# Fourier mixing and a gated feed-forward: the 481-column chunk goes first, and its half row tiles are joined over two batches

## The chip, the core and the metric

One core of a Trainium2 chip runs the kernel. The metric is the device time of one execution in microseconds (us). Engines are named as in the profile: PE is TensorE (matmuls; PEld its weight loads), DVE is VectorE, ACT is ScalarE, POOL is GpSimd, SP is SyncE, whose queue issues nearly all DMAs. SBUF is the on-chip memory, PSUM the small memory that matmuls write. POOL's work here lies in SBUF alone.

## The reference

The input `x` is 8 batches of 3008 tokens with 256 values. The reference mixes by a Fourier transform and sends every token through a gated feed-forward block:

```python
X = np.fft.fft(x, axis=1)
X = np.fft.fft(X, axis=2)
x = X.real.reshape(24064, 256)
g = x @ w_gate                              # 256 x 1536
gelu = 0.5 * g * (1.0 + erf(g / sqrt(2)))
out = (gelu * (x @ w_val)) @ w_out          # 1536 x 256
```

## The kernel before

**Half the tokens, twice used.** The transform is built so that token t and its mirror 3008 - t come from one column: an even part and an odd part, added for t (called plus) and subtracted for the mirror (minus). Instead of 3008 tokens the first layer therefore works on NCOL = 1505 columns of a tile Y with two planes. The channel transform is folded into the weights WE (even), WOP (odd) and WOM (odd, negated). Column 1504 is a token that is its own mirror: it has a plus and no minus.

**Chunks and units.** A batch's 1505 columns are cut into three chunks (line 73) of 512, 512 and 481 columns, in this order. The hidden dimension of 1536 is cut into 12 blocks. A unit is one chunk and one block, so a batch has 36 units and the run 288; units are counted from 0 within a batch below. In a unit PE runs five first-layer matmuls (six in the first chunk of batch 0): WE into the value bank ps_v, WOM of the unit before into its gate bank ps_g, WOP of the unit before into its value bank, and WE and WOP into this unit's gate bank. ACT takes the gelu twice, glp for plus and glm for minus.

**Who writes h.** The hidden values of a chunk go into a tile h of 12 blocks with 1024 columns each. h has two buffers, so a chunk's tile takes over that of the chunk before last. Units go in pairs, and a pair is finished in the unit behind it: `val_odd` (line 628) has DVE multiply glp with the value bank into the plus columns of h (two blocks, 128x1024), then DVE computes dv, the minus value, and `minus` (line 647) has POOL multiply glm with dv into the minus columns, mirrored. Ahead of these DVE has one `ev` per unit, which reads ps_v between its two matmuls. In the first chunk of batch 0 DVE writes the minus columns too. Plus columns start at 0 in a block and minus columns at 512, for all three chunks.

**The second layer.** `l2_steps` (line 659) makes the list of matmuls of a finished chunk: four windows of plus columns and then four of minus columns, each of up to 128 tokens and each with 12 matmuls (one per block) of 256 output columns. The 481 chunk's last plus window has 97 tokens and its last minus window 96. Two windows share a PSUM tile ps_o of 512 columns, which has one buffer; after a pair's 24th matmul `finish` (line 701) has ACT copy it to SBUF (osb, two buffers) and SP store it by runs of 32 rows. In the last chunk of the run the pairs go to ps_o, ps_d, ps_g and ps_g.

**The order.** Each engine runs its instructions in the order in which the program issues them, by the loop at line 817. A unit's body issues the first layer, then steps of the next batch's transform (`a_step`, `b_steps`, which ACT evacuates), and last `second(8)` (line 916): eight second-layer matmuls from the list. The list of chunk c is added in the unit behind its last one, after that unit's `minus`, and 96 matmuls last 12 units. So in units 12 to 23 of a batch the second layer of its first chunk runs under the first layer of its second chunk; in units 24 to 35 that of the second chunk; and in units 0 to 11 that of the last batch's third chunk. POOL's queue also holds the folding of later batches' input (`fold_x`), in some of the odd units.

The output columns of the transform reach Y in two evacuations per step, `evac_top` (line 533, columns 0 to 767) and `evac_rest` (line 541, columns from 768 on).

Of the kernel before, what the change touches and what calls it, by code (L numbers as in the profile page):

```python
# [10 lines left out]
BF16 = mybir.dt.bfloat16  # L11
AF = mybir.ActivationFunctionType
# [25 lines left out]
def kernel(  # L38
# [20 lines left out]
    nc = tc.nc  # L59
# [10 lines left out]
    NFC = F // 128  # L70
    NCOL = T // 2 + 1
    YW = NCOL + 1
    CH = [(0, 512), (512, 512), (1024, NCOL - 1024)]
    MID = 24

    const_pool = ctx.enter_context(tc.tile_pool(name="const", bufs=1))
# [18 lines left out]
    WNb = const_pool.tile([128, NFC], BF16)  # L95
    WN = const_pool.tile([128, NFC], FP32)
    NQs = [const_pool.tile([128, YW], BF16, name=f"nq{i}") for i in range(2)]
    xf_bufs = [const_pool.tile([128, HJ, 2, 128], BF16, name=f"xf{i}") for i in range(2)]

    Ap = const_pool.tile([128, NG, C], BF16)  # L100
# [88 lines left out]
    def ps_d():  # L189
        return psum.tile([128, 512], FP32, tag="d", bufs=1, name="ps_d")  # L190
# [307 lines left out]
    def b_steps(b, eo, q):  # L498
# [40 lines left out]
                _sub(ps, [[1, MID], [N2, 8]], 0))  # L539

        def evac_rest():
            ps, Y, g0 = box["ps"], Ys[b], 8 * q
            n2 = N2 - MID
            f = 1 if q == 0 else 0
            copy(
                _sub(Y, [[32, n2], [1, 8 - f]], eo * YW + 32 * MID + g0 + f - 1),
                _sub(ps, [[1, n2], [N2, 8 - f]], MID + f * N2))
            if q == 0:
                copy(
                    _sub(Y, [[32, n2]], eo * YW + 32 * MID + 31), ps[:, MID:N2])  # L550
                copy(
                    _sub(Y, [[1, 1]], eo * YW + NCOL - 1), ps[:, 8 * N2 : 8 * N2 + 1])

        steps = [mm(gi, False) for gi in range(8)]
        if eo == 1 and b == 0:
            steps += [mm(gi, True) for gi in range(8)]
        def evac():
            evac_top()
            evac_rest()

        return steps, evac, evac_top, evac_rest

# [12 lines left out]
    def open_unit(u):  # L575
        b, ci, fc = units[u]
        if fc == 0:
            hs[(b, ci)] = h_tile()
        c0, n = CH[ci]
        if u % 2 == 0:  # L580
            duos[u // 2] = dict(pv=ps_v(), glp=glp_tile(), glm=glm_tile(), log=[])
            if kind(u):
                duos[u // 2]["ev"] = ev_tile()
        banks[u] = dict(
            d=duos[u // 2], k=u % 2, pv=duos[u // 2]["pv"][:, u % 2, :],
            glp=duos[u // 2]["glp"][:, u % 2, :], glm=duos[u // 2]["glm"][:, u % 2, :],
            b=b, fc=fc, c0=c0, n=n, nm=n - n % 32, kd=kind(u), fs=slice(fc * 128, (fc + 1) * 128),
            h=hs[(b, ci)], Y=Ys[b], nq=NQs[b % 2])

    def layer1(r, ps, W, i, eo, n, start):  # L590
        m = pe.matmul(
# [31 lines left out]
    def plus(r):  # L623
        n = r["n"]
        apart(r["d"]["log"], r["k"], vec.tensor_tensor(
            r["h"][:, r["fc"], :n], r["glp"][:, :n], r["pv"][:, :n], op=ALU.mult))

    def val_odd(u):
        r = banks[u]
        n, nm, d = r["n"], r["nm"], r["d"]  # L630
        if r["kd"] == 0:
            layer1(r, r["pv"], WOM, 1, 1, nm, False)
            hm = _sub(r["h"], [[-1, nm]], r["fc"] * 1024 + 512 + nm - 1)
            apart(d["log"], r["k"], vec.tensor_tensor(
                hm, r["glm"][:, :nm], r["pv"][:, :nm], op=ALU.mult))
            return
        layer1(r, r["pv"], WOP, 1, 1, n, False)
        if r["k"]:
            f = r["fc"] - 1
            apart(d["log"], None, vec.tensor_tensor(  # L640
                r["h"][:, f : f + 2, :n], d["glp"][:, :, :n], d["pv"][:, :, :n], op=ALU.mult))
            d["dv"] = dv_tile()
            apart(d["log"], None, vec.scalar_tensor_tensor(
                d["dv"][:, :, :nm], d["ev"][:, :, :nm], 2.0, d["pv"][:, :, :nm],
                op0=ALU.mult, op1=ALU.subtract))

    def minus(u):
        r = banks.pop(u)
        if r["kd"] and r["k"]:
            nm, d = r["nm"], r["d"]  # L650
            hm = _sub(r["h"], [[1024, 2], [-1, nm]], (r["fc"] - 1) * 1024 + 512 + nm - 1)
            pool.tensor_tensor(hm, d["glm"][:, :, :nm], d["dv"][:, :, :nm], op=ALU.mult)

    def store(b, dst_row, t, p0, s0, ns, rows, step):
        dst = ap_replace(
            out, ap=[[C, rows], [step * C, ns], [1, C]], offset=out.offset + (b * T + dst_row) * C)
        nc.sync.dma_start(out=dst, in_=_sub(t, [[C, ns], [1, C]], s0 * C, p0, rows))

    def l2_steps(b, ci):

        last = (b, ci) == (B - 1, len(CH) - 1)
        c0, n = CH[ci]
        m0 = c0 // 32
        nm = n // 32
        steps = []
        for sign in range(2):
            for pair in range(2):
                box = {}
                for s in range(2):
                    sub = 2 * pair + s  # L670
                    M = min(128, (n if sign == 0 else 32 * nm) - sub * 128)
                    for fc in range(NFC):
                        def run(sign=sign, pair=pair, s=s, sub=sub, M=M, fc=fc, box=box):
                            if last and sign and pair and s and fc == 0:
                                box["ps"] = ps_d()
                            if "ps" not in box:
                                box["ps"] = (ps_o, ps_d, ps_g, ps_g)[
                                    2 * sign + pair if last else 0]()
                            ps = box["ps"]
                            h = hs[(b, ci)]  # L680
                            (pe.matmul(
                                ps[:M, s * C : (s + 1) * C],
                                h[:, fc, sign * 512 + sub * 128 : sign * 512 + sub * 128 + M],
                                Wo_sb[:, fc, :], start=(fc == 0), stop=(fc == NFC - 1)))
                            if last and sign and pair and fc == NFC - 1:
                                finish_half(s, M, box)
                            elif s == 1 and fc == NFC - 1:
                                finish(sign, pair, M, box["ps"])
                        steps.append(run)

        def finish_half(s, M, box):
            if s == 0:
                box["t"] = osb_tile()
            t, ps = box["t"], box["ps"]
            (act.copy, vec.tensor_copy)[s](t[:M, s, :], ps[:M, s * C : (s + 1) * C])
            r0 = 64 * (N2 - (m0 + nm - 1 - 8 - 4 * s)) - 32
            dst = ap_replace(
                out, ap=[[64 * C, M // 32], [C, 32], [1, C]], offset=out.offset + (b * T + r0) * C)
            (nc.scalar, nc.sync)[s].dma_start(out=dst, in_=t[:M, s, :])

        def finish(sign, pair, M, ps):
            t = osb_tile()
            if M == 128:
                (act.activation(_sub(t, [[1, 2 * C]], 0), ps, AF.Copy))
            else:
                (act.activation(t[:, 0, :], ps[:, :C], AF.Copy))
                (act.activation(t[:M, 1, :], ps[:M, C:], AF.Copy))
            for q in range(4):
                rb = 8 * pair + q
                both = rb + 4 < nm  # L710
                if sign == 0:
                    m = m0 + rb
                    store(b, 64 * m + (m >= MID), t, 32 * q, 0, 2 if both else 1, 32, 256)
                else:
                    m = m0 + nm - 1 - rb
                    r0 = 64 * (N2 - m) - (32 if m >= MID else 31)
                    if both and m - 4 == 0:
                        store(b, r0, t, 32 * q, 0, 1, 32, 256)
                        store(b, r0 + 256, t, 32 * q, 1, 1, 31, 256)
                    else:  # L720
                        store(b, r0, t, 32 * q, 0, 2 if both else 1, 32, 256)
            if sign == 0 and n % 32 and pair == 1:
                store(b, T // 2, t, n % 128 - 1, 1, 1, 1, 256)

        return steps

# [57 lines left out]
    for eo in range(2):  # L784
        for q in range(4):
            steps, evac, evac_top, evac_rest = b_steps(0, eo, q)
            for s in steps:
                s()
            if eo:
                evac_top()  # L790
                later_evacs.append(evac_rest)
            else:
                evac()
    cast_w(512)
# [22 lines left out]
    for u in range(NU + 2):  # L817
# [32 lines left out]
        if u == 0:  # L850
# [6 lines left out]
            for e in later_evacs:  # L857
                e()
            n_first(0)
            act.activation(r["glp"], r["pg"], AF.Gelu)  # L860
            plus(r)
        elif u < NU:
            val_even(u)
# [48 lines left out]
                        z_read(b + 1, (8, 10, 13).index(k))  # L912
        if 0 < u <= NU and u % 12 == 0:
            pb, pi = divmod(u // 12 - 1, 3)
            l2q += l2_steps(pb, pi)
        second(8 if u <= NU else len(l2q))


# [28 lines left out]
```

## Time and profile before

| what | value |
|---|---|
| runs of the kernel before (median of 3) | 636.64 us (635.9 to 636.69) |
| the profiled execution's span | 636.0 us |
| granted TensorE clock, mean | 0.996 |
| first-layer work starts at | 30.23 us |
| one batch of 36 units (batches 1 to 6) | 74.3 us; batch 1 starts at 103.55, batch 2 at 177.84 |
| DVE / ACT / POOL busy | 541.4 / 477.0 / 439.8 us |

The three runs and the span are from one kernel; the profile was taken in one execution, whose own span is 0.64 us below the median of the runs. Nearly all instructions carry line 25, that of the recording helper, so groups are told apart by tiles: `ps_o<-Wo_sb,h` is the second layer, `ps_v<-Y,WE` the first matmul of a unit, `h<-glp,ps_v` DVE's plus multiply, `h<-glm,dv` POOL's minus multiply, `osb<-ps_o` ACT's evacuation. A matmul's duration in the rows is from its start to its modelled end; matmuls overlap, so what one costs PE is the distance between two starts.

### The profile page before, as it was taken

How to read it: one execution, taken by the hardware profiler on the slowest of the kernel's cores; microseconds unless marked ns; L12 is line 12 of the kernel's file. 1: busy time of each engine (PE TensorE's matmuls, PEld its weight loads, DVE VectorE, ACT ScalarE, POOL GpSimd, SP SyncE). 2: the span in 40 equal slices, each digit the busy share in tenths (PEclk: the TensorE clock that was granted, in tenths of full speed). 3: DMA queues.
4: the chain of work that ended last, by engine and by line, in shares of the span. 5: the costliest groups of instructions: out<-in, count | busy, mean ns of one | idle time of the engine just before them, and what ended most of it. 6: DMA issues, size and time to landing. Idle time of an engine off the chain costs nothing.

```text
span 636.0 us, 13041 instructions
## 1 busy us (share of the span) xinstructions
PE 615.9 (97%) x4628; PEld 410.0 (64%) x4628; DVE 541.4 (85%) x654; ACT 477.0 (75%) x971; POOL 439.8 (69%) x448
## 2 busy tenths in 40 slices
PE   3899999999999999999999999999999999999996
PEld 2445666666666666666666666666666666666665
DVE  7688988898888988889888988889888998899991
ACT  7587787877788777887778777887778877767661
POOL 8394987768868688677777688686885455555551
PEclk9899999999999999999999999999999999999999
DMA  8995614553236522565235632366223511211113
GB/s 305 350 274 188 188 48 130 158 187 112 70 105 196 186 76 65 158 200 160 51 111 160 197 113 67 109 189 210 57 64 94 184 48 48 62 49 41 49 42 79
DMA packets 65401, 82.39 MB, mean 130 GB/s; under 512 B 8241, under 2 KB 58929, under 8 KB 62521
## 3 DMA queue, kind: packets, MB, share of 16 engines
q1 hardware_dynamic: 63653, 80.65, 40.8%
q0 software_dynamic: 1552, 0.79, 0.9%
q8 instruction: 36, 0.59, 0.4%
q14 instruction: 28, 0.23, 0.1%
q10 hardware_dynamic: 132, 0.13, 0.1%
HBM read 45.08 MB, written 37.25 MB: 129 GB/s over the span
## 4 chain that ended last, share of the span: by engine, by line
PE 93%; DVE 3%; DMA 1%; ACT 1%; POOL 0%; issue 0%; SPq 0%; ACTq 0%; DVEq 0%
PE ps_o L25 39%; PE ps_g L25 29%; PE ps_v L25 19%; PE ps_d L25 6%; DVE h L25 1%; DMA gate<-z 1%; DVE S L25 0%; DVE dv L25 0%; DMA out_dram<-osb 0%; ACT glp L25 0%; ACT S L25 0%; SPq L25 0%; DVE WOM L25 0%; ACT glm L25 0%; ACT osb L25 0%
## 5 line engine op out<-in xcount | busy, mean ns | idle before, releaser
L25 POOL TENSOR_TENSOR h<-glm,dv 128x1024 bf16<-128x1024 bf16 (+1 forms) x138 | 290.3, 2104 | 170.6 <-DVE dv L25 113.9
L25 PE MATMUL ps_o<-Wo_sb,h 128*128 128x256 bf16 (+2 forms) x2232 | 288.8, 272 | 0.4 <-ACT osb L25 0.3
L25 DVE SCALAR_TENSOR_TENSOR ev<-nq,WN,ps_v 128x512 f32<-128x512 bf16 (+1 forms) x276 | 202.4, 733 | 67.3 <-PE ps_v L25 45.4
L25 PEld LDWEIGHTS <-h 128*128 128x128 bf16 (+2 forms) x2304 | 222.8, 100 | 52.4 <-issue 0.8
L25 ACT ACTIVATE glm<-ps_g 128x512 bf16<-128x512 f32 (+1 forms) x288 | 169.4, 588 | 109.6 <-PE ps_g L25 79.3
L25 DVE TENSOR_TENSOR h<-glp,ps_v 128x1024 bf16<-128x1024 bf16 (+2 forms) x150 | 172.9, 1153 | 4.9 <-ACT glp L25 3.1
L25 ACT ACTIVATE glp<-ps_g 128x512 bf16<-128x512 f32 (+1 forms) x288 | 170.0, 590 | 8.8
L25 DVE SCALAR_TENSOR_TENSOR dv<-ev,ps_v 128x1024 f32<-128x1024 f32 (+1 forms) x138 | 164.5, 1192 | 0.0
L25 POOL TENSOR_TENSOR xf<-xin 128x254 bf16<-128x254 f32 x168 | 118.3, 726 | 0.3 <-DMA xin<-in_x_dram 0.3
L25 PE MATMUL ps_v<-Y,WE 128*128 128x512 bf16 (+1 forms) x288 | 108.0, 375 | 0.0
L25 PE MATMUL ps_g<-Y,WOM 128*128 128x512 bf16 (+1 forms) x288 | 107.7, 374 | 0.0
L25 PE MATMUL ps_v<-Y,WOP 128*128 128x512 bf16 (+1 forms) x288 | 107.7, 374 | 0.0
L25 PE MATMUL ps_g<-Y,WOP 128*128 128x512 bf16 (+1 forms) x288 | 107.6, 374 | 0.0
L25 PE MATMUL ps_g<-Y,WE 128*128 128x512 bf16 (+1 forms) x288 | 107.5, 373 | 0.0
L25 PEld LDWEIGHTS <-WOP 128*128 128x128 bf16 x576 | 55.7, 97 | 53.6 <-ACT WOP L25 0.4
L25 PEld LDWEIGHTS <-WE 128*128 128x128 bf16 x576 | 56.0, 97 | 30.6 <-issue 0.3
L25 ACT ACTIVATE osb<-ps_o 128x512 f32<-128x512 f32 (+2 forms) x107 | 56.5, 542 | 19.2 <-PE ps_o L25 16.4
L25 PEld LDWEIGHTS <-Ap 128*128 128x128 bf16 (+1 forms) x561 | 41.0, 96 | 31.6 <-issue 0.3
L25 ACT ACTIVATE S<-ps_d 128x512 bf16<-128x512 f32 x80 | 47.4, 592 | 0.2 <-PE ps_d L25 0.2
L25 PEld LDWEIGHTS <-G 128*128 128x128 bf16 x213 | 21.2, 101 | 35.7 <-issue 11.9
L25 ACT ACTIVATE Y<-ps_d 128x192 bf16<-128x192 f32 (+4 forms) x142 | 37.0, 341 | 0.4 <-PE ps_d L25 0.4
L25 PEld LDWEIGHTS <-WOM 128*128 128x128 bf16 x300 | 29.2, 97 | 5.1
(133 smaller groups left out, 243.2 us busy)
## 6 DMA issues: line engine op xcount, KB each, us to landing
out_dram<-osb SPq DMA_DIRECT2D x357, 64.0 KB
xin<-in_x_dram SPq DMA_DIRECT2D x16, 1024.0 KB
Ap<-z SPq DMA_DIRECT2D x24, 512.0 KB
xin<-in_x_dram SPq DMA_DIRECT2D x8, 896.0 KB
z<-S SPq DMA_DIRECT2D x7, 768.0 KB
z<-S SPq DMA_DIRECT2D x8, 512.0 KB
nq<-nrow SPq DMA_DIRECT2D x8, 376.2 KB
z<-S SPq DMA_DIRECT2D x11, 256.0 KB
```

Source lines behind the costliest of these rows:

```text
L25: return lambda *a, **k: self._tc.keep_in_program_order(call(*a, **k))
```

## The change

The 481 chunk is the first of each batch, and the order of Y's evacuations is turned round so that its columns come first. In the 481 chunk the minus columns now stand at 0 to 479 of each block of h and the plus columns at 480 to 960, without a hole; its 960 tokens (without the lone column) make seven windows of 128 and a rest of 64. POOL copies the rest of an even batch into one half of a spare tile (hx for eight blocks, the no longer used CW for four), that of the odd batch behind it into the other half, and the odd batch runs one joined window. So an even batch's 481 chunk has seven windows (the last alone in its PSUM tile) and an odd one's eight, instead of eight each: 188 windows instead of 192. All windows have 128 rows. The lone column, number 960 of the 481 chunk, is copied by POOL into column 1023 of the second chunk's h, a minus place that has no row of its own (token 0 has no mirror). `second` no longer takes eight steps but what is left of the list, divided by the units left until the next chunk.

```diff
-    CH = [(0, 512), (512, 512), (1024, NCOL - 1024)]
+    CH = [(1024, NCOL - 1024), (0, 512), (512, 512)]
...
+    HXF = NFC - NCH * 2
+    hx = const_pool.tile([128, HXF, 128], BF16)
...
         def evac():
+            evac_rest()
             evac_top()
-            evac_rest()
...
-            h=hs[(b, ci)], Y=Ys[b], nq=NQs[b % 2])
+            h=hs[(b, ci)], Y=Ys[b], nq=NQs[b % 2], po=0 if n == 512 else 480,
+            mo=512 if n == 512 else 0)
...
-            hm = _sub(r["h"], [[1024, 2], [-1, nm]], (r["fc"] - 1) * 1024 + 512 + nm - 1)
+            hm = _sub(r["h"], [[1024, 2], [-1, nm]], (r["fc"] - 1) * 1024 + r["mo"] + nm - 1)
             pool.tensor_tensor(hm, d["glm"][:, :, :nm], d["dv"][:, :, :nm], op=ALU.mult)
...
+    def windows(b, ci):
+        h = hs[(b, ci)]
+        c0, n = CH[ci]
+        m0, nb = c0 // 32, n // 32
+        ps = [plus_rows(b, m0 + i) for i in range(nb)]
+        ms = [minus_rows(b, m0 + nb - 1 - i) for i in range(nb)]
+        blocks = ps + ms if n == 512 else ms + ps
+        out = [(h, 128 * w, blocks[4 * w : 4 * w + 4], None) for w in range(len(blocks) // 4)]
+        if c0 == 0:
+            out[-1] = out[-1][:3] + (b * T + T // 2,)
+        if len(blocks) % 4:
+            left = blocks[-2:]
+            o = 64 * (b % 2)
+            pool.tensor_copy(hx[:, :, o : o + 64], h[:, :HXF, 896:960])
+            pool.tensor_copy(_sub(CW, [[128, NCH * 2], [1, 64]], o), h[:, HXF:, 896:960])
+            if b % 2:
+                out.append((None, 0, st[b - 1]["left"] + left, None))
+            else:
+                st[b]["left"] = left
+        return out
...
-        for sign in range(2):
-            for pair in range(2):
+        for w0 in range(0, len(ws), 2):
+            pair = ws[w0 : w0 + 2]
...
+                        if h is not None:
+                            w = h[:, fc, col : col + 128]
+                        elif fc < HXF:
+                            w = hx[:, fc, :]
+                        else:
+                            w = _sub(CW, [[1, 128]], 128 * (fc - HXF))
+                        pe.matmul(
+                            ps[:, s * C : (s + 1) * C], w,
+                            Wo_sb[:, fc, :], start=(fc == 0), stop=(fc == NFC - 1))
...
             if eo:
-                evac_top()
-                later_evacs.append(evac_rest)
+                evac_rest()
+                later_evacs.append(evac_top)
...
         if 0 < u <= NU and u % 12 == 0:
             pb, pi = divmod(u // 12 - 1, 3)
+            if CH[pi][0] == 0:
+                pool.tensor_copy(hs[(pb, pi)][:, :, 1023:1024], hs[(pb, pi - 1)][:, :, 960:961])
             l2q += l2_steps(pb, pi)
-        second(8 if u <= NU else len(l2q))
+        second(-(-len(l2q) // (12 - u % 12)) if u <= NU else len(l2q))
```

## The prediction

> **What bounds the kernel.** I read the busy table, then the chain that ended last, then the stages by windows and the single instructions by timeline.
>
> ```profile
> PE 615.9 (97%) x4628; PEld 410.0 (64%) x4628; DVE 541.4 (85%) x654; ACT 477.0 (75%) x971; POOL 439.8 (69%) x448
> ...
> PE 93%; DVE 3%; DMA 1%; ACT 1%; POOL 0%; issue 0%; SPq 0%; ACTq 0%; DVEq 0%
> ```
>
> TensorE (PE) holds 93% of the chain. A busy share can hide small gaps, so I looked at the stage that the change makes lighter: units 12 to 23 of a batch, where the second layer of the batch's first chunk runs. For batches 1 and 2 (columns: stretch, length, then busy time of PE, PEld, DVE, ACT, POOL, granted clock, DMA):
>
> ```profile
> 129.58:154.01 24.43, 24.43 (x186) 16.01 (x184) 22.01 (x24) 17.70 (x37) 17.82 (x17) 1.00 0.53 169
> 203.87:228.29 24.42, 24.42 (x185) 16.00 (x183) 22.01 (x24) 17.70 (x37) 17.85 (x17) 1.00 0.52 169
> ```
>
> PE is busy for the whole stage. A unit there takes 1.95 us: five first-layer matmuls 0.215 apart and eight second-layer ones 0.109 apart (starts 200.82 to 201.70 for eight). So a removed matmul is worth 0.109 us, and every wait put on PE here is lost in full.
>
> **Part 1, fewer matmuls: -5.25 us.** The built order has 2256 second-layer matmuls against 2304: 48 fewer, 48 x 0.109 = 5.25. A tile of 96 or 97 tokens costs PE what one of 128 does (272 to 273 ns each, same 0.109 spacing), so nothing else is saved. All 48 fall in units 12 to 23 of batches 0, 2, 4 and 6: 84 instead of 96, given out seven to a unit.
>
> **Part 2, the first window of the 481 chunk: +17.15 us.** Before, every chunk's second layer began with rows that DVE writes (plus), and came to the rows that POOL writes (minus) after 48 matmuls, six units later. Now the 481 chunk begins with minus rows. The built program shows the semaphore: the 11th matmul of the window, in unit 13, waits for POOL's multiply of units 10 and 11, which is only issued in unit 12. Batch 0 escapes (there DVE writes minus); batches 1 to 7 do not. When is that multiply done? The same 960-wide chain stands in the trace at the end of a 481 chunk, in the unit that starts at 177.84:
>
> ```profile
> 177.84 0.38 PE L25 MATMUL ps_v<-Y,WE 128*128 128x512 bf16 x1
> ...
> 178.26 0.37 PE L25 MATMUL ps_v<-Y,WOP 128*128 128x481 bf16 x1
> ...
> 178.93 1.15 DVE L25 TENSOR_TENSOR h<-glp,ps_v 128x962 bf16<-128x962 bf16 x1
> ...
> 179.99 1.15 DVE L25 SCALAR_TENSOR_TENSOR dv<-ev,ps_v 128x960 f32<-128x960 f32 x1
> ...
> 181.28 2.03 POOL L25 TENSOR_TENSOR h<-glm,dv 128x960 bf16<-128x960 bf16 x1 [0.39 <-ACT glm L25]
> ```
>
> POOL ends at 183.31, 5.47 us after the unit began. PE wants the data after unit 12 and the first layer of unit 13, two matmuls in: 1.92 + 1.08 + 2 x 0.109 = 3.22 us (the same at seven or eight to a unit). The semaphore and the weight load behind it (0.097 in the PEld rows) add some 0.2, so PE stands for 5.47 + 0.2 - 3.22 = 2.45 us; 2.3 to 2.5 between no and slow hand-over. Seven batches: 17.15. All of PE's queue stands behind that weight load, so the next unit's matmuls, and with them DVE, ACT and POOL, wait too.
>
> **Part 3, seven to a unit: +11.7 us.** A pair of windows is 24 matmuls in ps_o, which has one buffer. At eight to a unit a pair ended with a unit, and ACT emptied ps_o under the next unit's 1.08 us of first layer. At seven it ends in units 15, 18 and 22, after the third, sixth and second matmul, and the next matmul needs ps_o at once. What that costs is seen once, at the end of the run:
>
> ```profile
> 617.93 1.04 PE L25 MATMUL ps_o<-Wo_sb,h 128*128 128x256 bf16 x8
> ...
> 619.00 0.60 ACT L25 ACTIVATE osb<-ps_o 128x512 f32<-128x512 f32 x1 [0.30 <-PE ps_o L25]
> ...
> 619.65 2.78 PE L25 MATMUL ps_o<-Wo_sb,h 128*128 128x256 bf16 x24 [0.28 <-ACT osb L25]
> ```
>
> The last of the eight starts at 618.70, the next at 619.65: 0.95 instead of 0.109, a price of 0.85 with ACT free. In unit 15 ACT is in the gelu glp until it can take the next at 1.77 after the unit's start: osb to 2.37, PE at 2.42 instead of 1.41, 1.01. Units 18 and 22: 0.85 each. In batch 0, unit 22 first empties a batch-1 step (four Y copies, last start 2.34): PE at 3.15 instead of 1.40, 1.75. Sum: 3 x 2.71 + 3.61 = 11.7. Ends: 12 x 0.85 = 10.2, and 12.5 if ACT is late each time. Odd batches have 96 matmuls, eight to a unit, and pay nothing.
>
> **Part 4, the lone token: +7.4 us.** The 128x12 copy is queued on POOL in unit 24 behind the multiply of units 22 and 23. In the built program DVE's next h multiply (units 24 and 25, writing the buffer that the copy reads) waits for it. POOL's multiply ends 5.68 us after unit 24 began (233.97 against 228.29); that DVE multiply would start at about 5.2. No row has a copy of twelve lone elements; the nearest:
>
> ```profile
> L25 POOL CAST xf<-xin 128x4 bf16<-128x4 f32 x84 | 17.1, 203 | 0.0
> ...
> L25 POOL CAST xf<-xin 128x16 bf16<-128x16 f32 x3 | 2.9, 964 | 0.0
> ```
>
> 0.20 to 0.96, 50 to 60 ns a strided element; I take 0.60. [...] By the rows the copy ends at 5.7 + 0.1 + 0.6 = 6.4, DVE starts at 6.55, 1.35 late. Behind it DVE has dv and ev of unit 27, for which PE's WOP matmul in unit 28 waits. Today that ev ends 0.65 ahead in batches 1 to 6 (0.25 to 0.3 in batch 7); with 512 columns I allow 0.45 and 0.15. PE loses 0.9 six times, 1.4 in batch 7 and 0.6 in batch 0: 7.4. Ends: 3 (a copy of 0.2) to 10.3 (0.96).
>
> **Part 5, the clock: +6 us.** A stop of this length is in the trace before the kernel's main loop:
>
> ```profile
> 20.31 1.03 PE L25 MATMUL ps_d<-G 128*128 128x512 bf16 x4
> 23.74 3.40 PE L25 MATMUL ps_d<-G,gate 128*128 128x512 bf16 x8 [2.40 <-DMA gate<-z]
> ```
>
> ```profile
> 21.40:23.40 2.00, 0.00 (x0) 0.00 (x0) 1.63 (x6) 1.66 (x6) 0.00 (x0) 1.00 1.07 389
> 23.40:23.70 0.30, 0.00 (x0) 0.00 (x0) 0.00 (x0) 0.30 (x1) 0.00 (x0) 0.50 0.70 178
> 23.70:26.80 3.10, 3.06 (x8) 1.14 (x9) 0.75 (x1) 1.63 (x3) 0.00 (x1) 0.50 0.97 367
> 27.00:28.00 1.00, 1.00 (x42) 1.00 (x41) 0.60 (x4) 0.40 (x2) 0.84 (x1) 1.00 0.98 408
> ```
>
> After 2.40 us without a matmul the granted clock was 0.50 for 3.4 us. Part 2 makes seven such stops. If one drops the clock, 3.4 us of work run at half speed: 1.7 lost, about 1.5 where the stop reaches into the slow stretch. How the stop lies to whatever measures it decides; between none and seven I take four: 6 (0 to 11.9).
>
> **Costed at nothing.** The two POOL copies of left-over rows in unit 12 (768 elements; 1024 took 1.04 us) come behind the multiply that matters; POOL then idles until unit 14's dv. Without that cover they would delay POOL by 0.8 us per batch. Stores: 397 on SP in both programs. The 31 columns that move from units 24-35 to 0-11 cancel on PE, bound in both. Start-up: the larger of a step's evacuations goes first (+0.08 us), and twelve batch-0 matmuls shrink from 512 to 480 (-0.16).
>
> **Sum.** -5.25 + 17.15 + 11.7 + 7.4 + 6.0 = +37.0. The profiled execution spans 636.0, which makes 673.0; it stands 0.6 below the median of 636.64, so I predict 673.6.
>
> **Rivals.**
> - *The clock holds* (parts 1 to 4 alone): 636.64 + 31.0 = 667.6. For: one stop in this trace is thin evidence. Against: the row above. [...] Here 2.40 us was enough. Chance 0.27.
> - *Everything at its upper end* (all seven stops slow the clock, copy 0.96 us): 636.64 - 5.25 + 17.5 + 12.5 + 10.3 + 11.9 = 683.6; chance 0.15.
> - *One of the waits is hidden*: for instance POOL's chain ends 2 us sooner, leaving parts 1, 3 and 4: 650 to 660. Against: DVE's order fixes the chain. Chance 0.08.
> - *Faster*: the matmuls go and no wait replaces them, 631.4. Place: PE at the 11th matmul of the first minus window. It decides if POOL's multiply is done within 3.22 us of unit 12's start, and ps_o is emptied within 0.11. Against: 5.47, and 0.95. Chance 0.04.
>
> **From cases to numbers.** The forecast has 0.46. The range 659 to 684 takes in the first two rivals' times and the sum's low end (-5.25 + 16.1 + 10.2 + 3 = 660.7); it leaves out the faster case and parts of the second and third. A measurement here tells about 0.2% from no change: faster 0.04, within 0.01, slower 0.95.
>
> **What would show it.** PE waiting for POOL h some 2.4 us in unit 13 of batches 1 to 7, and not in batch 0; PE waiting for ACT osb three times in batches 0, 2, 4, 6, and none in odd ones; DVE h waiting for POOL in unit 26; the granted clock at 0.5 behind some stops; 2256 second-layer matmuls. A PE that stays full in units 12 to 24 would refute parts 2 and 3.

## The result

The changed kernel takes 668.39 us (median of 4 runs, 665.91 to 669.85) against 636.27 us before (635.59 to 636.69): 1.0491 of before, 95% interval 1.0472 to 1.051. It is slower, 5 us short of the forecast and inside its range.

The profiled execution of the changed kernel spans 666.7 us. Its busy table and its chain, from the page:

```profile
PE 617.9 (93%) x4522; PEld 404.5 (61%) x4580; DVE 542.1 (81%) x654; ACT 473.7 (71%) x956; POOL 449.2 (67%) x472
...
PE 78%; DVE 10%; POOL 5%; ACT 3%; issue 2%; DMA 1%; SPq 0%; ACTq 0%; DVEq 0%; POOLq 0%
```

PE's share of the chain fell from 93% to 78%, and POOL, which had none, holds 5%. The list of waits says for whom PE and DVE stood (columns: total us, times, longest):

```profile
PEld L25 <- POOL h L25: 16.8, 7, 2.4
PE ps_o L25 <- POOL h L25: 14.9, 7, 2.1
...
PE ps_o L25 <- ACT osb L25: 9.9, 13, 1.5
...
DVE h L25 <- POOL h L25: 5.3, 7, 0.8
```

The first two rows are one event, seen at the weight load and at the matmul behind it: seven stops, one for each of batches 1 to 7. The third has the twelve of the even batches and one more. None of these four rows stood for more than 0.3 us before.

**Stop one, POOL.** Timeline of batch 3, whose unit 12 begins at 287.75:

```profile
287.75 0.38 PE L25 MATMUL ps_v<-Y,WE 128*128 128x512 bf16 x1
...
288.83 1.15 DVE L25 TENSOR_TENSOR h<-glp,ps_v 128x962 bf16<-128x962 bf16 x1
...
289.89 1.15 DVE L25 SCALAR_TENSOR_TENSOR dv<-ev,ps_v 128x960 f32<-128x960 f32 x1
...
290.75 0.38 PE L25 MATMUL ps_o<-Wo_sb,h 128*128 128x256 bf16 x2
...
291.19 2.01 POOL L25 TENSOR_TENSOR h<-glm,dv 128x960 bf16<-128x960 bf16 x1 [0.72 <-DVE dv L25]
...
293.25 0.55 PEld L25 LDWEIGHTS <-h 128*128 128x128 bf16 x6 [2.40 <-POOL h L25]
293.26 0.83 PE L25 MATMUL ps_o<-Wo_sb,h 128*128 128x256 bf16 x6 [2.13 <-POOL h L25]
```

PE has issued two of unit 13's eight matmuls by 290.97, 3.22 us after unit 12 began. DVE's two steps and POOL's multiply run one behind the other to 293.20 (5.45 us), and PE goes on 0.06 us later: 2.29 us lost. The row's 2.13 is shorter because the last matmul's modelled end counts as busy.

**Stop two, ACT.** Batch 2, unit 15, three matmuls into the second layer:

```profile
218.30 0.49 PE L25 MATMUL ps_o<-Wo_sb,h 128*128 128x256 bf16 x3
218.50 0.60 ACT L25 ACTIVATE glp<-ps_g 128x512 bf16<-128x512 f32 x1
219.00 0.59 ACT L25 ACTIVATE osb<-ps_o 128x512 f32<-128x512 f32 x1
219.64 0.60 PE L25 MATMUL ps_o<-Wo_sb,h 128*128 128x256 bf16 x4 [0.84 <-ACT osb L25]
```

The fourth matmul would have started at 218.63; it starts at 219.64, when osb has left ps_o. 1.01 us.

**Stop three, DVE behind the lone copy.** Batch 3, unit 24 begins at 314.4. POOL's row and then DVE's:

```profile
318.02 2.14 POOL L25 TENSOR_TENSOR h<-glm,dv 128x1024 bf16<-128x1024 bf16 x1 [0.81 <-DVE dv L25]
320.22 0.24 POOL L25 COPY h<-h 128x12 bf16<-128x12 bf16 x1
```

```profile
320.50 1.22 DVE L25 TENSOR_TENSOR h<-glp,ps_v 128x1024 bf16<-128x1024 bf16 x1 [0.78 <-POOL h L25]
```

The copy takes 0.24, DVE waits 0.78 until it is through, and PE loses 0.35 of that in unit 28 (2.40 us instead of 2.05). The seven waits in the list are those of batches 0 to 6. In batch 7 DVE waits 0.98 us and goes on 0.03 after the copy, but the list puts that wait down to PE's ps_o; PE loses 0.87 there.

**The clock.** Stretches of batch 1, around its first stop (columns: stretch, length, busy PE, PEld, DVE, ACT, POOL, then the granted clock):

```profile
132.20:134.70 2.50, 0.38 (x4) 0.10 (x3) 0.90 (x2) 0.75 (x2) 2.12 (x2) 1.00 0.40 107
...
135.60:138.90 3.30, 3.30 (x13) 1.74 (x12) 2.96 (x3) 1.19 (x2) 0.00 (x0) 0.50 0.96 385
139.00:142.40 3.40, 3.35 (x22) 2.09 (x22) 1.86 (x4) 2.50 (x5) 2.14 (x1) 1.00 0.32 82
```

From 0.79 to 0.96 us after PE went on, the clock is 0.50 for 3.41 us: PE is busy all the time, with 13 matmul rows where the next stretch has 22. That happens behind four of the seven stops (batches 1, 2, 4 and 6), and costs 1.67 to 1.69 us each.

**The account.** Unit times, from the first weight load of each unit to that of the next, give each term its measured size:

| term | forecast | measured | how |
|---|---|---|---|
| 1, 48 matmuls fewer | -5.25 | -5.2 | units 12 to 23 without a stop: 1.84 for 1.95 |
| 2, first window waits for POOL | +17.15 | +16.1 | unit 13: 4.25 for 1.95, 4.14 for 1.84; 7 x 2.30 |
| 3, pairs that end inside a unit | +11.7 | +11.7 | batch 0: 1.01 + 0.87 + 1.69; others 3 x (1.01 + 0.87 + 0.84) |
| 4, lone copy | +7.4 | +3.0 | unit 28: 6 x 0.35, 0.87 in batch 7, nothing in batch 0 |
| 5, half-clock stretches | +6.0 | +6.7 | 4 x 1.68 |
| start-up | 0 | -1.55 | first layer starts at 28.68, not 30.23 |
| sum | +37.0 | +30.7 | spans: 666.7 - 636.0 = 30.7 |

The start-up row is chance: the execution profiled before has one half-clock stretch ahead of its first layer (the prediction shows it), the one profiled after has none, 1.00 from 23.4 to 26.8. Such a stretch seems to part the runs of before into two groups too: 635.6 to 636.8 us with a mean clock of 0.997 to 1.0, and 637.6 to 638.6 with 0.994 to 0.997. The profiled span of 636.0 is one of the second group (spans of 635.5 to 636.5; the first has 633.6 to 634.6). Between executions without it the difference is 32.2, close to the runs' 668.4 - 636.3 = 32.1.

Two differences that are no term of the table nearly cancel. Units 8 to 11 of batch 0 take 7.89 us instead of 8.90 in this execution, of which their 31 fewer columns explain some 0.3; in the profiled kernels with the new chunk order they vary between 7.88 and 8.97. And the end of the run, from the start of the last unit on, takes 19.79 us instead of 19.20.

### The profile page after: what moved, and what is told of

It is laid out like the page before. It is cut to its first block, busy times and chain, and to the rows that moved or that the text cites. A ratio compares the mean times of both kernels' runs of the same rounds, so it can differ in the third digit from the quotient of the medians.

```text
span 666.7 us, 12872 instructions
## 1 busy us (share of the span) xinstructions
PE 617.9 (93%) x4522; PEld 404.5 (61%) x4580; DVE 542.1 (81%) x654; ACT 473.7 (71%) x956; POOL 449.2 (67%) x472
## 4 chain that ended last, share of the span: by engine, by line
PE 78%; DVE 10%; POOL 5%; ACT 3%; issue 2%; DMA 1%; SPq 0%; ACTq 0%; DVEq 0%; POOLq 0%
PE ps_o L25 32%; PE ps_g L25 23%; PE ps_v L25 17%; PE ps_d L25 6%; POOL h L25 4%; DVE h L25 4%; DVE dv L25 4%; ACT osb L25 1%; DVE ev L25 1%; ACT glm L25 1%; DMA gate<-z 1%; ACT glp L25 1%; DVE S L25 0%; ACT S L25 0%; DMA out_dram<-osb 0%
## 5 line engine op out<-in xcount | busy, mean ns | idle before, releaser
L25 PE MATMUL ps_o<-Wo_sb,h 128*128 128x256 bf16 x2136 | 284.0, 274 | 25.2 <-POOL h L25 14.9
L25 PEld LDWEIGHTS <-h 128*128 128x128 bf16 x2208 | 211.8, 98 | 82.0 <-POOL h L25 16.8
L25 DVE TENSOR_TENSOR h<-glp,ps_v 128x1024 bf16<-128x1024 bf16 (+2 forms) x150 | 173.0, 1153 | 11.7 <-POOL h L25 5.3
L25 PE MATMUL ps_v<-Y,WE 128*128 128x512 bf16 (+1 forms) x280 | 105.7, 378 | 0.9 <-DVE dv L25 0.5
L25 PE MATMUL ps_g<-Y,WOP 128*128 128x512 bf16 (+1 forms) x275 | 103.8, 378 | 1.6
L25 PE MATMUL ps_g<-Y,WE 128*128 128x512 bf16 (+1 forms) x255 | 96.2, 377 | 0.0
L25 ACT ACTIVATE osb<-ps_o 128x512 f32<-128x512 f32 x93 | 54.8, 589 | 16.9 <-PE ps_o L25 13.2
L25 ACT ACTIVATE Y<-ps_d 128x192 bf16<-128x192 f32 (+4 forms) x142 | 34.0, 338 | 0.5 <-PE ps_d L25 0.5
```

Source lines behind the costliest of these rows:

```text
L25: return lambda *a, **k: self._tc.keep_in_program_order(call(*a, **k))
```

## The experiments

The theory: three waits (terms 2 to 4) and the clock behind the first make the time; the saved matmuls are worth what they were. The main rival: the join itself costs, by its copies on POOL, its narrower first chunk or its shifted columns, and the waits only show where PE happens to meet that. All times below are medians beside runs of the kernel before on the same chip (636.7 us).

### Plus windows first

```diff
         if len(blocks) % 4:
+            out = out[4:] + out[:4]
             left = blocks[-2:]
```

> The 481 chunk's windows are issued in another order: its pure plus windows (5th to 7th) first, the minus ones behind. Nothing else differs from the changed kernel (668.4 us). Theory (the 11th matmul waits for POOL's last minus multiply, and the stop sometimes halves the clock): unit 13 falls from 4.14-4.25 us to 1.84-1.95 in batches 1 to 7, no PE wait for POOL h, no half-clock stretch behind a stop; 7 x 2.30 + 4 x 1.69 = 22.9 us less, 645.5 us (643 to 648). Rival (POOL is simply late and PE meets it at a later matmul): a wait of the same total stays, at units 16 and 17, and the time stays over 660.

Measured: 645.68 us, 1.014 of before (1.0122 to 1.0157). Unit 13 takes 1.95 and 1.84 us, no wait of PE for POOL's h is left, and no half-clock stretch stands between start and end. Units 17 (odd batches) and 18 (even ones), where the first minus window now reaches its last blocks, keep their length: POOL is not late, it was only asked too early. One line of order was worth 22.7 us, over two thirds of the loss.

### Eight a unit

```diff
-        second(-(-len(l2q) // (12 - u % 12)) if u <= NU else len(l2q))
+        second(8 if u <= NU else len(l2q))
```

> Eight second-layer matmuls a unit again, in place of what is left divided by the units left; an even batch's list then ends in unit 22. Theory (a pair that ends inside a unit makes PE wait for ACT to empty ps_o): the waits in units 15, 18 and 22 of batches 0, 2, 4 and 6 go, 11.7 us less, 656.7 us (654 to 659, since the number of half-clock stretches can differ by one or two of 1.7 us). Rival (ps_o is waited for wherever the pair ends): three waits of 0.85 us stay in each even batch, within 2 us of 668.4.

Measured: 662.98 us, 1.0412 (1.0383 to 1.0441): 6 us more than expected, and more than the allowance. The three waits for ACT are gone, as the theory says (units 15 and 18 take 1.95 and 2.08 us). Two things were not foreseen. The clock: the profiled execution has five slow stretches behind stops and not four, and one at the start-up, together some 3.1 us; the four runs' mean clock is 0.978 to 0.985, where that of the changed kernel is 0.986 to 0.993. And DVE takes some 1.8 us back: an even batch's list is empty in unit 22, so that units 22 and 23 shrink to 1.98 and 1.27 us and unit 24 grows from 2.05 to 2.50. (Another 0.7 lies in units 8 to 11 of batch 0, which vary.) The windows of batch 2 in the kernel with all three undone, which has the same pace, show why: units 21 and 22, then 23 and 24:

```profile
217.39:221.32 3.93, 3.93 (x34) 2.41 (x32) 3.49 (x5) 3.40 (x8) 3.77 (x5) 1.00 0.71 257
221.32:225.08 3.76, 3.55 (x29) 2.09 (x26) 3.76 (x5) 2.83 (x8) 3.31 (x4) 1.00 0.14 36
```

In the first stretch PE is full and DVE is not; in the second DVE is busy for all of its 3.76 us and PE waits: there DVE sets the pace. Its four operations for a pair of units take 3.57 us where they stand back to back (65.75 to 69.32 in the even-pace kernel below), more than the 3.25 of units 22 and 23.

### The lone column by a tile of its own

```diff
+    lone = const_pool.tile([128, NFC, 1], BF16)
...
+            pool.tensor_copy(lone[:, :, :], h[:, :, 960:961])
...
-                pool.tensor_copy(hs[(pb, pi)][:, :, 1023:1024], hs[(pb, pi - 1)][:, :, 960:961])
+                pool.tensor_copy(hs[(pb, pi)][:, :, 1023:1024], lone[:, :, :])
```

> The lone column goes to a small tile of its own in unit 12 (a POOL copy behind the two of the left-over rows) and from there into column 1023 in unit 24, so that DVE's first multiply into the reused buffer no longer waits for POOL. Theory: unit 28 falls from 2.40 to 2.05 us in batches 1 to 6 and from 2.82 to 1.95 in batch 7, together 3.0 us less, 665.4 us, with the half-clock stretches as likely as before. Rival (the wait only uses up slack that PE does not need): no change beyond the stretches, 668.4.

Measured: 665.80 us, 1.045 (1.0419 to 1.048); the interval overlaps that of the changed kernel, since the runs lie between 662.6 and 669.6 with the number of slow stretches. The median alone would not settle it. The units do: unit 28 takes 2.05 and 1.95 us in place of 2.40 and 2.82, in every batch, and DVE's wait for POOL's h is gone from the list of waits. 3.0 us, against the rival.

### Part of the stop filled

Four matmuls whose results nothing uses are run inside the wait:

```diff
+            if pb and pi == 0:
+                new[10] = lambda s=new[10]: (warm(4), s())
```

> Four idle matmuls of 512 columns (results unused) are put ahead of the 11th matmul of the 481 chunk's first window in batches 1 to 7, inside the wait for POOL: the wait ends when it did, but PE idles some 1.3 us of it and not 2.17. Theory (the clock halves when PE idles 2.17 us or more in one 3.41 us window, and does not at 1.58): unit 13 stays at 4.14 to 4.25 us, no half-clock stretch behind it, 4 x 1.69 = 6.8 us less than the profiled 666.7, some 661.5 for the median (660 to 663), and the runs lie closer together. Rival (the slow stretches come from something else than the idle time, or the extra matmuls cost 0.86 us each time): 668 or, with the cost, 674.

Measured: 662.25 us, 1.0394 (1.0377 to 1.0412), the runs within 1.7 us. Unit 13 takes 4.25 and 4.14 us as before, so the stop is as long; but PE idles 1.26 us of it at most, by the rows, where it idled 2.13 in the changed kernel. (The expectation's 2.17 and 1.58 are a little high. By the rows, the changed kernel's stops put 2.12 or 2.13 us into one 3.41 us window where the clock halved, and 1.50 or less where it did not.) Batch 1, the rest of the stop and the stretch behind it:

```profile
132.70:134.00 1.30, 0.09 (x1) 0.00 (x0) 0.00 (x0) 0.00 (x0) 1.30 (x2) 1.00 0.08 19
134.10:137.40 3.30, 3.30 (x23) 2.20 (x24) 2.27 (x3) 1.73 (x4) 0.79 (x2) 1.00 0.98 367
```

The clock stays at 1.00. Work that nobody needs made the kernel 6.1 us faster, which is term 5, near enough.

### Minus windows first, in the kernel before

```diff
-        for sign in range(2):
+        for sign in ((1, 0) if ci == 2 and not last else (0, 1)):
```

> The kernel before, with one thing altered: the 481 chunks of batches 0 to 6 (third in their batch here) issue their minus windows first. Nothing is joined or copied and the chunks keep their order. Theory (the order of the windows alone makes the wait): PE stops in unit 1 of batches 1 to 7 until POOL has written the last minus pair, 5.47 us after unit 0 began plus 0.05; it arrives at 2.14 + 1.30 + 0.22 = 3.66 (3.23 in batch 7), so 6 x 1.86 + 2.29 = 13.5 us more, 650.1 us (648.5 to 652, a half-clock stretch behind the longest stop included or not). Rival (the wait came from the join, its copies on POOL or the new chunk order): within 1 us of before.

Measured: 651.33 us, 1.0229 (1.0206 to 1.0252). Without any join, copy or new chunk order the stop is there: unit 1 takes 4.03 us instead of 2.17 in batches 1 to 6, 4.32 instead of 1.95 in batch 7. POOL and PE in batch 2:

```profile
183.25 2.02 POOL L25 TENSOR_TENSOR h<-glm,dv 128x960 bf16<-128x960 bf16 x1 [0.39 <-ACT glm L25]
...
185.32 0.83 PE L25 MATMUL ps_o<-Wo_sb,h 128*128 128x256 bf16 x6 [1.69 <-POOL h L25]
```

And the two lengths of stop part on the clock, batch 6 (1.69 us idle) above batch 7 (2.13):

```profile
491.50:494.90 3.40, 3.40 (x27) 2.48 (x26) 3.17 (x4) 3.35 (x7) 0.74 (x1) 1.00 0.09 21
...
566.60:569.90 3.30, 3.30 (x13) 1.50 (x12) 2.16 (x3) 1.19 (x2) 0.00 (x0) 0.50 0.00 0
```

### All three waits undone

> The changed kernel with all three waits undone together: plus windows first in the 481 chunk, eight matmuls a unit, the lone column by its own tile. Theory (the change's own worth is 48 matmuls of 0.109 us, and all that made it slower are the three waits and the clock behind the first): 636.6 - 5.2 and 1.6 given back in units 22 to 24 of even batches, where DVE cannot follow the lighter units (0.4 us each time with eight a unit), 633.0 us (632 to 634), faster than before by 0.5%. Rival (the joined window and the copies cost something of their own): 636 or more.

Measured: 635.17 us (12 runs), 0.9959 of before (0.9944 to 0.9974): faster, but by 1.6 and not 3.7, and so between the expectation's 632 to 634 and its rival's 636. The runs lie from 632.6 to 636.1 and differ in their clock: those with a mean clock of 0.999 take 632.6 to 633.5, and before takes 635.8 to 636.8 where it has 0.999 or 1.0. Like with like the gain is some 3.2 us, near the 3.6 that the expectation had. That most of the others among the 12 runs have a half-clock stretch at the start is inferred from their lower mean clock; only an execution without one was traced.

### All three undone, at an even pace

```diff
-        second(8 if u <= NU else len(l2q))
+        second((6 if b % 2 == 0 and 18 <= i < 24 else 8) if u <= NU else len(l2q))
```

> As the kernel with all three undone, but the 84 matmuls of an even batch are given out eight a unit in units 12 to 17 and six a unit in units 18 to 23, so that pairs still end with a unit and no unit runs out of second-layer work. Theory: unit 24 falls from 2.50 to 2.05 us, units 18 to 23 are 0.22 shorter each, the whole 5.2 us come out: 631.4 us (630.5 to 632.5). Rival (DVE's own pace of some 3.75 us a pair of units takes the gain wherever it is put): no better than eight a unit, 633.

Measured: 632.83 us, 0.993 (0.9909 to 0.995), the fastest of all, but 0.3 over the expectation's allowance and, as a median, next to its rival's 633. Three of the six runs have a clock of 0.995 or 0.996 and take 633.3 to 633.5. The other three take 631.6 to 632.4 with 0.998, some 4.5 us under before's 636.3. The busy table:

```profile
PE 609.7 (97%) x4580; PEld 402.2 (64%) x4580; DVE 541.7 (86%) x654; ACT 472.3 (75%) x956; POOL 450.1 (71%) x480
```

Units 18 to 23 of batches 2, 4 and 6 take 0.22 us less each (0.19 in unit 22), unit 24 is 2.05 to 2.06, and PE is busy for 97% of the span, as before. There the rival falls, since units 18 and 19, and 20 and 21, take 3.68 to 3.70 us a pair, with PE busy all the time.

The profiled execution, the slowest of the three, shows where the rest is. Without the start-up it is 4.1 us shorter than before, so that 1.1 of 5.2 are missing. Some 0.6 are lost in batch 0, whose units 18 to 23 give 0.70 and not 1.3: DVE has no pause from 65.75 to 72.33 there, so that the rival holds in units 19 and 20 (3.70 us together instead of 3.46), and in unit 21 PE stands for 0.36 until a DMA into Ap has landed. Another 0.4 lies behind the start of the last unit (19.64 us for 19.20). All profiled kernels with the new chunk order have such a longer end, 19.6 to 20.0, and the kernel before with minus windows first has not, 19.20; so it comes with the order or the join. Beside a loss of 32 us that is all that is left of the main rival.

## Why the prediction was right, and where not

- **Parts 1 and 3** came out to a tenth: -5.2 and +11.7. Reading ACT's queue at the point where each pair ends (behind the gelu, free, behind four Y copies) gave three different prices, forecast as 1.01, 0.85 and 1.75 and measured as 1.01, 0.84 to 0.87 and 1.69.
- **Part 2** had the right mechanism, place and batches: 2.30 a stop in place of 2.45. The step "the semaphore and the weight load behind it add some 0.2" was too dear; POOL's end and PE's weight load are 0.05 apart, and the matmul follows in 0.01.
- **Part 4** is the term that was mis-sized, 7.4 for 3.0. "I take 0.60" failed: the copy took 0.239 us. Both rows in the prediction cast fp32 to bf16, but the 16-element one stands in the start-up, and the one of 84 times 0.203 was the better neighbour. Why 16 elements take 0.96 stays open. The part's low end, 3 for a copy of 0.2, is what came: a copy of 0.239, and 3.0. With 0.24 the same working gives some 1.0 us of lateness for DVE, of which 0.78 was measured; the slack of 0.45 was allowed about rightly (0.78 of waiting, 0.35 lost), and so was the 0.15 of batch 7 (0.98 and 0.87). The forecast's own working has a slip: 1.35 late less 0.15 of slack is 1.2 for batch 7, not 1.4, and its 0.6 for batch 0 has no working at all; there DVE waited 0.58 and PE lost no more than 0.05.
- **Part 5**, four stretches, was the middle of an open range, and four was a draw: other executions of the same kernel have mean clocks from 0.986 to 0.993. The rival "the clock holds" gives 667.6, nearer to the median than the forecast, and is still wrong: the stretches are there, and the profile's clock rows and the filled stop show what they cost. It came close by luck: parts 4 and 2 were together 5.5 too dear, nearly what the stretches cost (6.7).
- **The sum's own base**: the span of 636.0 belongs to an execution with a half-clock stretch at its start. A run's time stands 1.7 to 2.3 us over its span, and 2.1 to 2.2 for the kernel before, so that execution would read about 638, and the median of 636.64 that the sum was added to belongs to the other group. The 0.6 that the forecast added to get from the span to the median was no such distance. That is the -1.55 of the account.

What stays open: why the end of the run is 0.4 to 0.8 us longer with the new chunk order, and why units 8 to 11 of batch 0 vary.

## What to carry to other kernels

When work is reordered to save instructions on a full engine, look at the first thing that the new order asks for and at which engine produces it last: here one window order cost three times what the saved matmuls were worth, and one line gave it back. Make groups that share a single-buffered accumulator end where the engine has other work, and spread a saving so that no stretch falls under the next engine's own pace. A saved row on a full engine counts only once every wait in its neighbourhood has been priced at that engine's position, not by shares of busy time.

## What the runs showed of the hardware that was not expected

In the profiled executions of before and of the changed kernel, all changes of the granted clock lie on a grid of 3.413 us. In the changed kernel they stand at 12.66, 135.54, 138.95, 214.05, 217.46 and 371.06 us and so on, which is 36, 1, 22, 1 and 45 such intervals apart; in the kernel before at 13.16, 23.40, 26.81 and 634.38, which is 3, 1 and 178.

Over the profiled executions of five kernels PE stopped for POOL 35 times, seven times in each, and fifteen of these stops were followed by one interval at half clock: four in the changed kernel, five each with eight a unit and with the lone column's own tile, one in the kernel before with minus windows first, none with the stops part filled. The place of the stop counted as well as its length. By the rows the changed kernel's seven stops are equally long, 2.12 or 2.13 us of idle PE. Those of batches 1, 2, 4 and 6 lie whole in one interval of the grid, and half clock followed; those of batches 3, 5 and 7 straddle a grid line, with 1.42, 1.50 and 1.33 us as their larger parts, and the clock stayed at 1.00. Shorter stops fit: 1.69 us (batch 6 with minus windows first) and 1.26 us (part filled) left the clock alone. So do the two start-ups: before, 2.05 us of the 2.40 us stop at 21.34 lie in one interval, and half clock followed; after, the stop of 2.42 us at 21.27 straddles a grid line, no interval holds more than 1.68 us, and it did not.

The grid's place differs between the two executions: the first change to full clock stands at 13.16 us before and at 12.66 after (the starts of matmuls of 256 columns go from 0.21 to 0.11 us apart there), though PE's first matmul starts at 8.74 and 8.67. That this is also why runs of one program have more or fewer slow intervals is likely, but not shown, since each program was traced once. The four runs with the stops cut to 1.26 us of idle time lie within 1.7 us; the six of the lone-column kernel, with stops of 2.13 us, within 7.0.
